# A transposing load for two chunks of x, and two weight loads moved to ScalarE's queue, in the start of a two-problem attention kernel

## Chip, cores, metric

One core of a Trainium2 chip. The metric is the device time of one execution in microseconds (us). "Span" is the time from the first to the last instruction in the profiled execution; it is 1.8 to 2.0 us shorter than the time of the same run. All runs told here were in the fast state (a granted TensorE clock of 0.998 to 1.0 of full speed over the run).

## The reference

Two independent problems A and B with equal shapes, their results side by side:

```python
q = (x @ wq).reshape(B, Sq, Hq, Dh).transpose(0, 2, 1, 3)      # x 16x32x1024, wq 1024x4096
k, v = repeat(k_cache, 8, axis=1), repeat(v_cache, 8, axis=1)  # caches 16x4x512x128
p = softmax(einsum("bhqd,bhkd->bhqk", q, k) * Dh ** -0.5)
out = einsum("bhqk,bhkd->bhqd", p, v).transpose(0, 2, 1, 3).reshape(B, Sq, Hq * Dh) @ wo
```

All data are bfloat16. Here only the first projection of problem A counts: 512 tokens, x split into eight chunks of 128 columns (chunk 0 to 7), and the first eight of 32 heads.

## The kernel before

The projection's matmuls read a chunk of x transposed, 128 columns on the partitions and 512 tokens along the row (128x512 in the trace). Before, chunks 0 to 3 come by plain loads and are transposed on TensorE (four 128x128 blocks each), then copied from PSUM by VectorE or ScalarE; chunks 4 to 7 come by two transposing loads. The queue order is the order of these lines; `NF` is 6, `HC` is 4, `TT` is 4.

```python
load_x(0, TT // 2, TT, nc.scalar)                             # chunks 0, 1, tokens 256..511
nc.scalar.preload_act_table_set("natural_log_exp_and_others")
load_x(0, 0, TT // 2)                                         # chunks 0, 1, tokens 0..255
load_w0(0, 1, 0, NF // 2)       # weights of chunk 0, heads 0..2
load_w0(0, 1, NF // 2, NF)      # weights of chunk 0, heads 3..5
load_w0(1, 2, 0, NF)            # weights of chunk 1
load_x(2, 0, TT)                # chunks 2, 3 of x
load_w0(2, 3, 0, NF)            # weights of chunk 2
load_w0(3, 4, 0, NF)            # weights of chunk 3
load_w0(0, HC, NF, REP)         # heads 6, 7 of chunks 0..3
# ... later loads cut
warm_up(22)                     # idle matmuls until x is there
for k, ts in enumerate(((0, TT // 2), (TT // 2, TT))):
    transpose_x(0, *ts, nc.vector.tensor_copy)
    transpose_x(1, *ts, nc.scalar.copy, spare[k])
for ts in ((0, TT // 2), (TT // 2, TT)):
    first_heads(range(0, NF // 2), (0,), *ts)     # six 256-column matmuls
first_heads(range(NF // 2, NF), (0,))             # three of 512 columns
first_heads(range(0, NF - 2), (1,))
transpose_x(2, 0, TT, nc.vector.tensor_copy)
transpose_x(3, 0, TT, nc.scalar.copy)
first_heads(range(NF - 2, NF), (1,))
first_heads(range(NF), (2, 3))
# ... then heads 6 and 7 of chunks 0..3, chunks 4..7, and the long stream of scores and projections
```

Of the kernel before, what the change touches and what calls it, by code (L numbers as in the profile page):

```python
# [16 lines left out]
P = 128  # L17
# [164 lines left out]
def kernel(  # L182
# [14 lines left out]
    nc = tc.nc  # L197
# [5 lines left out]
    TT = NTOK // P  # L203
# [14 lines left out]
    def fast_path(ok_i):  # L218
        with ExitStack() as fctx:
# [17 lines left out]
            def blk_tile(shape, name, dtype=BF16):  # L237
                return blk.tile(shape, dtype, name=name, tag="blk")
# [215 lines left out]

            NF = REP - 2
            HC = DC // 2
            x_sb = blk_tile([P, TT, HC * P], "x_sb")
            xT[0] = blk_tile([P, DC, NTOK], "xT")
            qT[0, 0] = blk_tile([P, B, REP, SQ], "qT")
            w0 = [blk_tile([P, HC, REP * DH], "w0_sb") for _ in range(2)]  # L460
            x_v = A_x.flatten_outer_dims().rearrange("(t p) d -> p t d", p=P)
            wq_v = A_wq.rearrange("(c p) n -> p c n", p=P)

            def load_x(d0, t0, t1, eng=nc.sync):
                eng.dma_start(
                    out=x_sb[:, t0:t1, d0 * P:(d0 + 2) * P],
                    in_=x_v[:, t0:t1, d0 * P:(d0 + 2) * P],
                )

            def load_x_transposed(d0):  # L470
                nc.sync.dma_start_transpose(
                    out=xT[0][:, d0:d0 + 2, :],
                    in_=A_x.flatten_outer_dims()[:, d0 * P:(d0 + 2) * P],
                )

            def load_w0(d0, d1, h0, h1):
                nc.sync.dma_start(
                    out=w0[d0 // HC][:, d0 % HC:(d1 - 1) % HC + 1, h0 * DH:h1 * DH],
                    in_=wq_v[:, d0:d1, h0 * DH:h1 * DH],
                )  # L480

            load_x(0, TT // 2, TT, nc.scalar)
            nc.scalar.preload_act_table_set("natural_log_exp_and_others")
            load_x(0, 0, TT // 2)
            load_w0(0, 1, 0, NF // 2)
            load_w0(0, 1, NF // 2, NF)
            load_w0(1, 2, 0, NF)
            load_x(2, 0, TT)
            load_w0(2, 3, 0, NF)
            load_w0(3, 4, 0, NF)  # L490
            load_w0(0, HC, NF, REP)
            load_w0(HC, HC + 1, 0, REP)
# [27 lines left out]
            def transpose_x(d, t0, t1, copy, ps=None):  # L520
                if ps is None:
                    ps = psum.tile([P, NTOK], BF16, name="xT_ps", tag="ob")
                for tt in range(t0, t1):
                    nc.tensor.transpose(  # L524
                        ps[:, tt * P:(tt + 1) * P], x_sb[:, tt, d * P:(d + 1) * P], ident[:]
                    )
                ts = slice(t0 * P, t1 * P)
                copy(out=xT[0][:, d, ts], in_=ps[:, ts])

            def first_heads(heads, dcs, t0=0, t1=TT):  # L530
                ts = slice(t0 * P, t1 * P)
                for dc in dcs:
                    for h in heads:
                        nc.tensor.matmul(  # L534
                            first_q[h][:, ts],
                            lhsT=w0[dc // HC][:, dc % HC, h * DH:(h + 1) * DH],
                            rhs=xT[0][:, dc, ts],
                            start=(dc == 0 and t0 == 0),
                            stop=(dc == DC - 1),
                        )  # L540
# [5 lines left out]
            for ts in ((0, TT // 2), (TT // 2, TT)):  # L546
                first_heads(range(0, NF // 2), (0,), *ts)
            first_heads(range(NF // 2, NF), (0,))
            first_heads(range(0, NF - 2), (1,))
            transpose_x(2, 0, TT, nc.vector.tensor_copy)  # L550
            transpose_x(3, 0, TT, nc.scalar.copy)
            first_heads(range(NF - 2, NF), (1,))
            first_heads(range(NF), (2, 3))
            first_q += [psum.tile([P, NW], FP32, name="q_ps", tag="ob")[:] for _ in range(2)]
            first_heads(range(NF, REP), range(HC))
            first_heads(range(REP), range(HC, DC - 1))
            for n, h in enumerate((0, 2, 4, 6, 5, 7, 1, 3)):
# [3 lines left out]
                    out=qT[0, 0][:, :, h, :],  # L561
                    in_=first_q[h].rearrange("p (b s) -> p b s", s=SQ),
# [91 lines left out]
            for k, (lim, op) in enumerate(((1.0 / SUM_HI, ALU.is_ge), (1.0 / SUM_LO, ALU.is_le))):  # L654
                nc.vector.tensor_scalar(
                    out=flags, in0=rall[0:QD].rearrange("p j n -> p (j n)"),
# [18 lines left out]
    ok_i = flag.tile([1, 1], I32, name="ok_i")  # L675
    total = 2 * 2 * NG * QW
    ok = fast_path(ok_i)
    with tc.If(ok < total, preferred_fallthrough_block=True, label="general"):
        general_path(tc, problems, out_flat)
# [30 lines left out]
```

## Time and profile before

| | before |
|---|---|
| time, median (first three runs, then all six of the comparison) | 343.63, then 343.60 us (343.02 to 343.73) |
| profiled run | 343.01 us, span 341.22 us |
| TensorE busy | 335.2 us, 98% of the span |
| chunk 4's first matmul starts at | 12.00 us |

### The profile page before, as it was taken

What the parts mean: (1) busy time and instruction counts of PE and PEld (TensorE: products, weight loads), DVE (VectorE), ACT (ScalarE), POOL (GpSimd) and SP (SyncE); (2) the same over time, 40 slices, a digit from 0 to 9 for tenths busy, and PEclk for the clock granted to TensorE, in tenths of its full rate; (3) what the DMA queues carried; (4) which work ended last, traced back from release to release, by engine and by line L of the source; (5) the groups of instructions that cost most, each with busy time, mean ns of one, the idle gap of its engine ahead of it and who ended that gap; (6) DMA issues with size and microseconds to landing.
All of it is one profiled execution on the core that took longest, in us unless ns stands there. A gap on an engine that the chain in (4) does not pass through costs nothing.

```text
span 341.2 us, 5454 instructions
## 1 busy us (share of the span) xinstructions
PE 335.2 (98%) x2082; PEld 213.6 (63%) x2121; DVE 265.5 (78%) x336; ACT 185.9 (54%) x209; POOL 46.7 (14%) x206
## 2 busy tenths in 40 slices
PE   8999999999999999999999999999999999999996
PEld 6455666666666666666666666666666666666555
DVE  1046988888988898888888988879888888889540
ACT  3058666666667667666645545555555555555110
POOL 0001110011111111110012221222122101111100
PEclk9999999999999999999999999999999999999999
DMA  7999999999996987899999955998449997430001
GB/s 211 287 190 273 285 249 202 233 242 268 291 248 154 232 242 219 210 314 299 308 306 258 250 125 144 334 268 242 118 103 296 356 187 176 104 97 16 18 18 33
DMA packets 128094, 71.70 MB, mean 210 GB/s; under 512 B 75840, under 2 KB 127296, under 8 KB 128064
## 3 DMA queue, kind: packets, MB, share of 16 engines
q1 hardware_dynamic: 127264, 70.07, 84.1%
q0 software_dynamic: 384, 1.05, 0.9%
q8 instruction: 17, 0.28, 0.3%
q10 hardware_dynamic: 416, 0.20, 0.2%
q14 instruction: 13, 0.11, 0.1%
HBM read 50.86 MB, written 2.10 MB: 155 GB/s over the span
## 4 chain that ended last, share of the span: by engine, by line
PE 98%; issue 1%; ACT 0%; ACTq 0%
PE f_ps L320 32%; PE q_ps L301 28%; PE ob L425 17%; PE s_ps L357 16%; PE q_ps L534 4%; PE q_ps L516 1%; PE xT_ps L524 0%; ACT o_sb L329 0%; ACTq L329 0%
## 5 line engine op out<-in xcount | busy, mean ns | idle before, releaser
L365 ACT ACTIVATE p_sb<-s_ps,shift 128x1024 bf16<-128x1024 f32 x128 | 142.7, 1115 | 97.5 <-PE s_ps L357 88.1
L376 DVE TRANSPOSE_TENSOR_REDUCE parts<-p_sb 128x32 f32<-128x1024 bf16 x128 | 158.7, 1240 | 21.0 <-ACT p_sb L365 19.3
L320 PE MATMUL f_ps<-wo_sb,oT 128*128 128x512 bf16 (+1 forms) x525 | 128.2, 366 | 0.6
L301 PE MATMUL q_ps<-xT,wq_sb 128*128 128x512 bf16 x430 | 113.2, 379 | 0.5
L425 PE MATMUL ob<-p_sb,v_sb 128*128 128x256 bf16 x512 | 76.8, 273 | 0.8
L357 PE MATMUL s_ps<-qT,kT 128*128 128x256 bf16 x512 | 76.8, 273 | 0.0
L320 PEld LDWEIGHTS <-oT 128*128 128x128 bf16 x544 | 53.2, 98 | 35.3
L357 PEld LDWEIGHTS <-kT 128*128 128x128 bf16 x512 | 56.9, 113 | 28.3
L301 PEld LDWEIGHTS <-wq_sb 128*128 128x128 bf16 x448 | 43.8, 98 | 32.2
L425 PEld LDWEIGHTS <-v_sb 128*128 128x128 bf16 x512 | 50.1, 98 | 20.0
L447 DVE TENSOR_TENSOR oT<-r,ob 128x512 bf16<-128x512 f32 x64 | 43.9, 686 | 19.9 <-PE ob L425 19.4
L411 DVE STREAM_TRANSPOSE r<-rall 128x512 f32<-128x512 f32 x64 | 44.2, 691 | 1.1
L309 ACT CAST qT<-q_ps 128x512 bf16<-128x512 f32 x56 | 32.7, 583 | 16.5 <-PE q_ps L301 16.5
L394 POOL COPY half<-cs 64x32 f32<-64x32 f32 x32 | 6.5, 204 | 231.8 <-DVE cs L384 231.8
L329 ACT CAST o_sb<-f_ps 128x512 bf16<-128x512 f32 (+1 forms) x17 | 9.5, 559 | 23.6 <-PE f_ps L320 23.6
L534 PE MATMUL q_ps<-xT,w_sb 128*128 128x512 bf16 (+1 forms) x65 | 14.4, 379 | 0.1
L384 DVE TENSOR_REDUCE cs<-parts 128x32 f32<-128x128 f32 x32 | 12.1, 377 | 1.1
L406 DVE RECIPROCAL rall<-sums 128x32 f32<-128x32 f32 x32 | 10.2, 319 | 3.3 <-POOL sums L403 3.3
L534 PEld LDWEIGHTS <-w_sb 128*128 128x128 bf16 x67 | 6.8, 102 | 7.0 <-DMA w_sb<-in_A_wq_dram 0.2
L560 DVE CAST qT<-q_ps 128x512 bf16<-128x512 f32 x4 | 2.5, 684 | 10.2 <-PE q_ps L534 10.2
L331 POOL DMA_DIRECT2D out_dram<-o_sb x8 | 4.6, 574 | 29.3 <-ACT o_sb L329 29.3
L395 POOL TENSOR_TENSOR half<-half,cs 64x32 f32<-64x32 f32 x32 | 7.8, 243 | 2.6
(25 smaller groups left out, 44.7 us busy)
## 6 DMA issues: line engine op xcount, KB each, us to landing
v_sb<-in_A_v_cache_dram SPq DMA_DIRECT2D x16, 512.0 KB, 5.7
wq_sb<-in_B_wq_dram SPq DMA_DIRECT2D x8, 1024.0 KB, 5.7
wo_sb<-in_A_wo_dram SPq DMA_DIRECT2D x8, 1024.0 KB, 7.4
v_sb<-in_B_v_cache_dram SPq DMA_DIRECT2D x16, 512.0 KB, 4.7
wo_sb<-in_B_wo_dram SPq DMA_DIRECT2D x8, 1024.0 KB, 8.1
wq_sb<-in_A_wq_dram SPq DMA_DIRECT2D x5, 1024.0 KB, 5.8
wq_sb<-in_A_wq_dram SPq DMA_DIRECT2D x2, 512.0 KB, 6.7
kT<-in_A_k_cache_dram SPq DMA_TRANSPOSE x64, 4.4
```

The costliest lines, as they stand in the source:

```text
L301: nc.tensor.matmul(ps[:], lhsT=w[:, dc, (h % 4) * DH:(h % 4 + 1) * DH], rhs=xT[pr][:, dc, :], start=(dc == 0), stop=(dc == DC - 1),)
L309: nc.scalar.copy(out=qT[pr, g][:, :, hl, :], in_=ps[:].rearrange("p (b s) -> p b s", s=SQ),)
L320: nc.tensor.matmul(ps[:, 0:width], lhsT=oT[pr, tt][:, h, :], rhs=wo_tiles[pr, nh, h // REP][:, h % REP, off:off + width], start=(h == 0), ...
L357: nc.tensor.matmul(s_ps[:, c, :], lhsT=kT[:, i % GRP, c, :], rhs=qT[pr, g][:, b, :, :].rearrange("p h s -> p (h s)"), start=True, stop=True,)
L365: nc.scalar.activation(out=p_sb[:], in_=s_ps[:], func=ACTF.Exp, bias=shift[:], scale=SCALE)
L376: nc.vector.tensor_reduce(out=parts[k][:, q, :, :].rearrange("p c h -> p (c h)"), in_=st[i]["p"][:].rearrange("p c (h s) -> p (c h) s", s=SQ),
L384: nc.vector.tensor_reduce(out=cs[:], in_=parts.pop(k)[:].rearrange("p q c h -> p q h c"), axis=AX.X, op=ALU.add,)
L406: nc.vector.reciprocal(out=rall[:, k, :], in_=quad.pop(k)[:])
L411: nc.vector.transpose(out=r[:].rearrange("p n s -> p (n s)"), in_=rall[:, k, o * 2 * REP:(o + 1) * 2 * REP] .unsqueeze(2).to_broadcast([P, ...
L425: nc.tensor.matmul(ob[j][:, q, :], lhsT=v_sb[:, i % GRP, c, :], rhs=st[i]["p"][:, c, :], start=(c == 0), stop=(c == KC - 1),)
L447: nc.vector.tensor_tensor(out=out, in0=rcp.pop(j)[:].rearrange("p (q h) s -> p q h s", h=REP), in1=ob.pop(j)[:].rearrange("p q (h s) -> p ...
L534: nc.tensor.matmul(first_q[h][:, ts], lhsT=w0[dc // HC][:, dc % HC, h * DH:(h + 1) * DH], rhs=xT[0][:, dc, ts], start=(dc == 0 and t0 == 0 ...
```

## The change

The intent: take eight transposes off TensorE, which is the bound. Chunks 2 and 3 come transposed by the DMA. Since that load keeps SyncE busy longer, ScalarE issues the weights of chunks 1 and 2.

```diff
-load_w0(1, 2, 0, NF)
-load_x(2, 0, TT)
-load_w0(2, 3, 0, NF)
+load_w0(1, 2, 0, NF, nc.scalar)
+load_x_transposed(2)
+load_w0(2, 3, 0, NF, nc.scalar)
 load_w0(3, 4, 0, NF)
 ...
-first_heads(range(0, NF - 2), (1,))
-transpose_x(2, 0, TT, nc.vector.tensor_copy)
-transpose_x(3, 0, TT, nc.scalar.copy)
-first_heads(range(NF - 2, NF), (1,))
-first_heads(range(NF), (2, 3))
+first_heads(range(NF), (1, 2, 3))
```

The rest of the diff halves `x_sb` to two chunks, so that `load_x` no longer names one, and gives `load_w0` an engine argument.

More of the change, by code (lines that the diff above doesn't have):

```diff
@@ L456, in fast_path @@
             HC = DC // 2
-            x_sb = blk_tile([P, TT, HC * P], "x_sb")
+            x_sb = blk_tile([P, TT, 2 * P], "x_sb")
             xT[0] = blk_tile([P, DC, NTOK], "xT")
@@ L462, in fast_path, with load_x @@
             wq_v = A_wq.rearrange("(c p) n -> p c n", p=P)
-            def load_x(d0, t0, t1, eng=nc.sync):
-                eng.dma_start(
-                    out=x_sb[:, t0:t1, d0 * P:(d0 + 2) * P],
-                    in_=x_v[:, t0:t1, d0 * P:(d0 + 2) * P],
-                )
+            def load_x(t0, t1, eng=nc.sync):
+                eng.dma_start(out=x_sb[:, t0:t1, :], in_=x_v[:, t0:t1, 0:2 * P])
             def load_x_transposed(d0):
@@ L474, in load_x_transposed, with load_w0 @@
                 )
-            def load_w0(d0, d1, h0, h1):
-                nc.sync.dma_start(
+            def load_w0(d0, d1, h0, h1, eng=nc.sync):
+                eng.dma_start(
                     out=w0[d0 // HC][:, d0 % HC:(d1 - 1) % HC + 1, h0 * DH:h1 * DH],
@@ L480, in load_w0 @@
                 )
-            load_x(0, TT // 2, TT, nc.scalar)
+            load_x(TT // 2, TT, nc.scalar)
             nc.scalar.preload_act_table_set("natural_log_exp_and_others")
-            load_x(0, 0, TT // 2)
+            load_x(0, TT // 2)
             load_w0(0, 1, 0, NF // 2)
             load_w0(0, 1, NF // 2, NF)
-            load_w0(1, 2, 0, NF)
-            load_x(2, 0, TT)
-            load_w0(2, 3, 0, NF)
+            load_w0(1, 2, 0, NF, nc.scalar)
+            load_x_transposed(2)
+            load_w0(2, 3, 0, NF, nc.scalar)
             load_w0(3, 4, 0, NF)
```

## The prediction

> **What bounds the kernel now.** I read the page first (busy shares, then the chain that ended last), then the chain and the timeline of the first 25 us, since the change touches nothing later, then the landing time of each early load.
>
> The busy line and the chain of the page:
>
> ```profile
> PE 335.2 (98%) x2082; PEld 213.6 (63%) x2121; DVE 265.5 (78%) x336; ACT 185.9 (54%) x209; POOL 46.7 (14%) x206
> ...
> PE 98%; issue 1%; ACT 0%; ACTq 0%
> ```
>
> TensorE carries 98% of the chain of a 341.2 us span. So a microsecond taken off TensorE's work, or put before it as a wait, in the first 10 us moves the end by that microsecond, unless a later wait takes it back. The chain in the first 25 us, in order of time (start, length, what):
>
> ```profile
> 3.45 0.92 PE xT_ps L524 x8
> 4.37 2.58 PE q_ps L534 x13
> 6.95 0.45 PE xT_ps L524 x8
> 7.40 0.05 issue
> 7.45 10.76 PE q_ps L534 x49
> ```
>
> All pieces are work; the one hole is 0.05 us. The third piece is what the change deletes: the eight transposes of chunks 2 and 3 of x (counting from 0). The first eight (chunks 0 and 1) stay. Next, the loads in the timeline (start, length of the issue, queue), with the rows of the engines that use them:
>
> ```profile
> 0.74 0.45 SPq L465 DMA_DIRECT2D x_sb<-in_A_x_dram  x1
> 0.82 0.46 ACTq L465 DMA_DIRECT2D x_sb<-in_A_x_dram  x1
> 1.26 1.39 SPq L477 DMA_DIRECT2D w_sb<-in_A_wq_dram  x3
> 1.31 1.28 ACT L483 ACT_TABLE_LOAD   x1 [1.31 <-PEq L694]
> 2.69 0.43 SPq L465 DMA_DIRECT2D x_sb<-in_A_x_dram  x1
> 3.17 2.00 SPq L477 DMA_DIRECT2D w_sb<-in_A_wq_dram  x4
> 5.21 1.52 SPq L471 DMA_TRANSPOSE xT<-in_A_x_dram  x1
> 5.79 0.67 PEld L534 LDWEIGHTS <-w_sb 128*128 128x128 bf16 x4 [0.20 <-DMA w_sb<-in_A_wq_dram]
> ```
>
> SyncE issues one plain load every 0.47 us, a transposing load of the same 256 KB in 1.52 us. The last row is the weight load of chunk 1: it came 0.20 us late behind its DMA, but the matmul before was still running, so TensorE lost nothing. The start is just in time: every load lands shortly before its use. From the trace, landing against need (us from the start of the span):
>
> - weights of chunk 0, heads 0 to 2: 3.92 against 4.06
> - weights of chunk 0, heads 3 to 5: 5.03 against 5.17
> - weights of chunk 1: 5.75 against 5.79
> - x of chunks 2 and 3: 6.55 against 6.59
> - weights of chunk 2: 7.06 against 7.45
> - weights of chunk 3: 7.77 against 8.77
> - heads 6 and 7 of chunks 0 to 3: 9.13 against 10.06
> - transposed chunks 4 and 5: 11.05 against 12.00
> - transposed chunks 6 and 7: 13.22 against 15.46
>
> [...] the chain's eight cold transposes take 0.92 us with a wait in them, the eight warm ones 0.45 us (56 ns each). What is deleted runs warm, so it is the cheap half.
>
> [...] between 3.5 and 4.7 us the DMA moved 77 to 215 GB/s, against 312 to 389 GB/s between 4.7 and 6.5 us, while SyncE was still feeding it 96 KB per 0.47 us (about 209 GB/s, an estimate from these rows).
>
> [...] at 22.57 us: a semaphore instruction of ScalarE's sequencer runs while its 0.59 us cast, begun at 22.56, is still busy.
>
> **The change, part by part.**
>
> Removed from TensorE: eight transposes. The next matmul started at 7.237; without them it would follow the one at 6.573 by one 512-column slot of 0.216 us, at 6.789. That is 7.237 - 6.789 = 0.45 us. Chunk 2's first matmul then waited 0.02 us for VectorE's copy (7.690 instead of 7.451 + 0.216 = 7.667). Together 0.47 us, all on the path: this is the ceiling of the gain, 0.14% of 343.63 us.
>
> Removed from VectorE and ScalarE: one copy each (0.42 and 0.59 us). Both engines idle 2.7 us before them and about 10 us after, so nothing.
>
> Removed from SyncE: three issues (0.43 + 0.43 + 0.50 us). Added: one transposing load at about 2.22 us, for 1.52 us as its twin shows. The next issue (weights of chunk 3) comes at 3.8 us, against 3.71 before: SyncE's later stream hardly shifts.
>
> Added to ScalarE: two issues of 0.45 us. If its sequencer runs on past the 1.28 us table load, as I expect from the 22.57 us case, they go out at about 1.35 and 1.85 us, ahead of the 2.22 and 3.17 us they had. If it waits for the table, at 2.6 and 3.1 us, or only after the transposing load's 1.52 us. ScalarE's next work (copies of chunk 1 at 3.92 us) is not reached either way.
>
> New waits. TensorE now wants chunk 1's second half at once, chunk 2 at 7.22 us instead of 7.69. When does the transposing load land? Ahead of it lie the weights of chunks 0, 1 and 2: 96 + 96 + 192 + 192 = 576 KB, 590 kB. From 3.2 us, where x is nearly in, at 340 GB/s (middle of the good stretch) that is 1.7 us; add 0.4 us for slow packets like those the trace has at 4.1 to 4.6 us: 5.3 us. Then 262 kB at 281 GB/s (what the second transposing load moved while alone, 11.6 to 12.4 us): 0.9 us. Then the last packets' way to the semaphore: 0.7 us (that load's packets ended at about 12.5, it landed at 13.22). Sum 7.0 us, uncertain by 0.5 either way, against 7.22. The first transposing load before had its packets stand for up to 1.2 us until 9.72, when the load ahead of it was ending (landed 9.89): so I let it land about 1 us after the last load ahead, not earlier.
>
> Second new wait: chunk 1's weights, pulled forward, share the DMA engines with chunk 0's second half, whose slack is 0.14 us. I allow 0.1 to 0.3 us of wait.
>
> Sum where ScalarE runs ahead: -0.47 + 0.2 (chunk 0) + 0.1 (transposing load, 0.3 late in one case of three) = about -0.2 us. Where ScalarE waits for its table: chunk 1's weights land 0.4 to 0.9 us late, so -0.47 + 0.4 to 0.9 = 0 to +0.4 us. I weigh 7 to 3: about -0.1 us, so 343.5 us.
>
> **The rivals.**
>
> (a) The full gain, 343.2 us: all loads in time. For it: ScalarE's issues fill the thin stretch at 3.5 to 4.7 us, and the weights of chunks 1 and 2 come sooner. Against it: slacks of 0.04 to 0.14 us and a load that is slow by nature as the new wait.
>
> (b) The transposing load takes the place of what it removes: both old ones needed 5.8 us from issue to landing. From 2.22 us that gives 8.0 us, 0.8 after the need: net +0.35, 344.0 us. Against it: those two queued behind four to six loads that had still to land; this one has fewer bytes ahead.
>
> (c) ScalarE's weights are late (table[...]): landing 3.5 us after an issue at 3.75 is 7.2 us, 1.4 after the need of 5.8: net +0.95, 344.6 us.
>
> (d) The loss is hidden or the gain given back later: chunks 4 and 5 have a slack of 0.95 us, less the 0.47 that TensorE comes sooner, so 0.48; heads 6 and 7 have 0.46. Enough if the stream is not late by half a microsecond; it carries the same bytes, only some 0.2 to 0.3 us slower for the transposed ones.
>
> **Range and chances.** The gain is capped at 0.47 us, the three runs before span 0.17 us: lower end 342.9. The loss is open to about +0.8 (b, half of c): upper end 344.4. Two per cent is 6.9 us; nothing in a 10 us start with waits of at most 1.5 us comes near it: faster 0.01, same 0.98, slower 0.01.
>
> **What would show it.** Right: the first 25 us of the chain have one transposing piece instead of two; ScalarE's two issues stand inside the table load; chunk 2's first matmul starts between 7.2 and 7.6; the transposing load lands between 6.6 and 7.6. Wrong on the high side: a hole of half a microsecond or more in TensorE before chunk 1 (ScalarE's weights) or before chunk 2 (the transposing load), or ScalarE's issues only at 2.6 us or later, or lengthened beyond 0.5 us. Wrong on the mechanism: a new hole after 9 us, at heads 6 and 7 or at chunk 4.

The sum: -0.47 + 0.2 + 0.1, about -0.2 us, against 0 to +0.4 us, weighed 7 to 3, came to about -0.1 us, so 343.5 us. "Cold" and "warm" are before and after the moment at which the trace records the full clock, 5.09 us here: the transposes stand 0.107 us apart before it, 0.056 us after. That ScalarE might issue only after the transposing load (2.22 + 1.52, about 3.75 us, the start of (c) with its +0.95 us and so of part of the upper end) was a possibility; no trace shows it. Two phrases are estimates that rest on its own lines: "slow by nature" in (a) on the 1.52 us issue against 0.43 to 0.50 for a plain one, and "0.2 to 0.3 us slower" in (d) on 281 GB/s against 340 to 389, which for 262 kB is 0.16 to 0.26 us.

## The result

Over six runs each: 343.09 us (342.66 to 343.60) against 343.60 us (343.02 to 343.73). Ratio 0.9989, 95% interval 0.9976 to 1.0002. A ratio here is the mean time of one kernel's fast runs over that of the other's of the same rounds, so not quite the ratio of the medians. The class is "same". The same kernel was run twice more among the experiments, at 0.9999 and 1.0002; the mean of the three ratios is 0.9997, which is -0.1 us. A gain is not established.

The profile after, of its fastest run (342.66 us). The page, busy line and chain:

```profile
PE 336.7 (99%) x2113; PEld 213.0 (62%) x2113; DVE 265.2 (78%) x335; ACT 185.4 (54%) x208; POOL 46.7 (14%) x206
...
PE 99%; ACT 0%; issue 0%; ACTq 0%
```

The chain of the first 25 us, in order of time:

```profile
3.45 0.95 PE xT_ps L521 x8
4.40 0.84 PE q_ps L531 x6
5.24 0.01 issue
5.25 13.36 PE q_ps L531 x61
```

The second piece of transposes is gone. Where it stood the matmuls run on. (TensorE's busy time in the page rises all the same, 335.2 to 336.7 us, because the trace of before lacks some matmul records: 2082 of them against 2121 weight loads, and 2113 of each after. The eight are seen in the weight loads.) The timeline of the queues and the weight loads (start, length):

```profile
0.82 0.46 ACTq L465 DMA_DIRECT2D x_sb<-in_A_x_dram  x1
...
1.25 0.93 SPq L474 DMA_DIRECT2D w_sb<-in_A_wq_dram  x2
1.31 1.28 ACT L480 ACT_TABLE_LOAD   x1 [1.31 <-PEq L687]
1.34 0.94 ACTq L474 DMA_DIRECT2D w_sb<-in_A_wq_dram  x2
2.22 1.33 SPq L468 DMA_TRANSPOSE xT<-in_A_x_dram  x1
...
5.24 4.67 PEld L531 LDWEIGHTS <-w_sb 128*128 128x128 bf16 x23 [0.29 <-DMA w_sb<-in_A_wq_dram]
```

ScalarE's two issues start at 1.34 us, while its table load (1.31 to 2.59) still runs. The transposing load is issued in 1.33 us and lands at 7.19; chunk 2's first matmul starts at 7.23, against 7.69 before. A new wait stands at 5.24: the second half of chunk 0's weights landed at 5.20, against 5.03 before, and TensorE was ready earlier.

Chunk 4 starts at 11.54 instead of 12.00 us, and from there the two traces run in parallel to the end: every score matmul that I compared comes 0.46 us earlier, the span ends 0.45 us earlier. It looks as if this one run had nearly the whole 0.47 us; the account below shows that it hadn't, and the next traces why not every run is as fast.

### The profile page after: what moved, and what is told of

Read it like the earlier page. It is cut to its first block, busy times and chain, and to the rows that moved or that the text cites. A ratio compares the mean times of both kernels' runs of the same rounds, so it can differ in the third digit from the quotient of the medians.

```text
span 340.8 us, 5475 instructions
## 1 busy us (share of the span) xinstructions
PE 336.7 (99%) x2113; PEld 213.0 (62%) x2113; DVE 265.2 (78%) x335; ACT 185.4 (54%) x208; POOL 46.7 (14%) x206
## 4 chain that ended last, share of the span: by engine, by line
PE 99%; ACT 0%; issue 0%; ACTq 0%
PE f_ps L320 32%; PE q_ps L301 28%; PE s_ps L357 16%; PE ob L425 16%; PE q_ps L531 4%; PE q_ps L513 1%; PE xT_ps L521 0%; ACT o_sb L329 0%; ACTq L329 0%
## 5 line engine op out<-in xcount | busy, mean ns | idle before, releaser
L320 PE MATMUL f_ps<-wo_sb,oT 128*128 128x512 bf16 (+1 forms) x544 | 132.3, 366 | 0.0
L301 PE MATMUL q_ps<-xT,wq_sb 128*128 128x512 bf16 x448 | 116.9, 379 | 0.0
L309 ACT CAST qT<-q_ps 128x512 bf16<-128x512 f32 x56 | 32.7, 583 | 16.5 <-PE q_ps L301 16.5
L553 ACT CAST qT<-q_ps 128x512 bf16<-128x512 f32 x4 | 2.1, 599 | 12.3 <-PE q_ps L531 12.3
```

Source lines behind the costliest of these rows:

```text
L301: nc.tensor.matmul(ps[:], lhsT=w[:, dc, (h % 4) * DH:(h % 4 + 1) * DH], rhs=xT[pr][:, dc, :], start=(dc == 0), stop=(dc == DC - 1),)
L309: nc.scalar.copy(out=qT[pr, g][:, :, hl, :], in_=ps[:].rearrange("p (b s) -> p b s", s=SQ),)
L320: nc.tensor.matmul(ps[:, 0:width], lhsT=oT[pr, tt][:, h, :], rhs=wo_tiles[pr, nh, h // REP][:, h % REP, off:off + width], start=(h == 0), ...
```

## The experiments

A common account helps to read them. Between chunk 0's first matmul and chunk 4's stand six 256-column and 29 512-column matmuls. At the full clock they take 0.109 and 0.216 us each from start to start, 6.91 us in all. What a trace shows beyond that is (a) the time from chunk 0's first matmul until TensorE gets its full clock: 256-column matmuls stand 0.21 us apart before and 0.11 us after, so half of that time is extra; the trace records when the clock was granted; (b) the transposes; (c) waits, as the rest. "Wait before" is the hole between the last transpose of chunks 0 and 1 and chunk 0's first matmul. Here for twelve traces, in us:

| kernel | wait before | clock granted at | (a) half clock | (b) transposes | (c) waits | chunk 4 starts | span |
|---|---|---|---|---|---|---|---|
| before | 0.00 | 5.09 | 0.46 | 0.47 | 0 | 12.00 | 341.22 |
| before, again (e11) | 0.00 | 5.44 | 0.68 | 0.47 | 0 | 12.14 | 341.36 |
| changed | 0.01 | 4.64 | 0.22 | 0 | 0.21 | 11.54 | 340.77 |
| changed, again (e4) | 0.49 | 6.13 | 0.78 | 0 | 0 | 12.24 | 341.48 |
| changed, third (e12) | 0.32 | 4.75 | 0.09 | 0 | 1.00 | 12.57 | 341.80 |
| e1 ScalarE's issues alone | 0.06 | 5.29 | 0.53 | 0.47 | 0.90 | 13.03 | 342.24 |
| e2 transposing load alone | 0.00 | 4.65 | 0.28 | 0 | 1.49 | 12.77 | 342.01 |
| e3 eight put back | 0.34 | 5.15 | 0.36 | 0.45 | 0.27 | 12.42 | 341.65 |
| e5 later transposing load | 0.48 | 3.91 | 0 | 0 | 0.83 | 12.28 | 341.51 |
| e7 queues exchanged | 0.00 | 5.05 | 0.47 | 0 | 0.29 | 11.78 | 341.01 |
| e10 chunk 2 held back | 0.00 | 5.12 | 0.51 | 0 | 0.81 | 12.32 | 341.70 |
| e13 one queue | 0.00 | 6.29 | 1.04 | 0 | 0 | 12.15 | 341.39 |

Read with it, the first trace of the change is partly luck. Its start is 0.46 us shorter than before by 0.47 for the transposes and 0.24 for an earlier clock, less 0.21 of new waits and 0.03 because chunk 0 began later: the earlier clock hid the waits.

And when the weights of chunk 0 (heads 0 to 2, heads 3 to 5), 1 and 2 and the transposing load landed:

| kernel | chunk 0, 0-2 | chunk 0, 3-5 | chunk 1 | chunk 2 | chunks 2, 3 of x |
|---|---|---|---|---|---|
| before | 3.92 | 5.03 | 5.75 | 7.06 | 6.55 (plain) |
| before, again | 3.79 | 4.95 | 5.73 | 7.36 | 6.48 (plain) |
| changed | 4.16 | 5.20 | 5.01 | 6.11 | 7.19 |
| changed, again | 4.53 | 5.44 | 4.75 | 5.72 | 6.59 |
| changed, third | 4.52 | 6.25 | 5.10 | 6.51 | 7.37 |
| e7 | 3.94 | 4.25 | 6.12 | 6.36 | 7.22 |
| e10 | 3.83 | 4.80 | 6.66 | 6.68 | 7.63 |
| e13 | 4.03 | 5.00 | 6.07 | 6.64 | 7.68 |

Twelve experiments ran, all with right results, each timed in five rounds (the number e9 is not used). The first four (e1 to e4) shared one chip and its runs of the kernel before (median 343.48), so did e5 to e8 (343.32), and e10 to e12 (343.47); e13 came last (343.30).

### e1: ScalarE's issues alone

```diff
 # on the kernel before
-load_w0(1, 2, 0, NF)
+load_w0(1, 2, 0, NF, nc.scalar)
 load_x(2, 0, TT)
-load_w0(2, 3, 0, NF)
+load_w0(2, 3, 0, NF, nc.scalar)
```

> The kernel before with one part of the change: ScalarE issues the weights of chunks 1 and 2; x of chunks 2 and 3 is still a plain load and is still transposed on TensorE. Theory (the gain is the 0.47 us of the removed transposes and their wait, the two issues only make it possible): nothing is gained, the eight transposes still stand in TensorE's row for 0.45 us, first score matmul at 22.3 to 22.6 us as before, time within 0.2 us of before. Rival (the earlier weights are the gain): first score matmul 0.3 us or more earlier, 343.1 us or less.

Measured: 344.12 us, ratio 1.0021 (1.0007 to 1.0035). Slower by 0.7 us, which neither theory said. The timeline of TensorE's weight loads:

```profile
4.22 0.99 PEld L534 LDWEIGHTS <-w_sb 128*128 128x128 bf16 x6
6.29 1.19 PEld L534 LDWEIGHTS <-w_sb 128*128 128x128 bf16 x7 [1.09 <-DMA w_sb<-in_A_wq_dram]
```

Chunk 0's second half landed at 6.25, not 5.03, while chunk 1's weights, which nobody wants before 5.8, were there at 4.74. Moving the two issues to ScalarE is by itself a loss: it put a later need ahead of an earlier one.

### e2: the transposing load alone

```diff
 # on the changed kernel
-load_w0(1, 2, 0, NF, nc.scalar)
+load_w0(1, 2, 0, NF)
 load_x_transposed(2)
-load_w0(2, 3, 0, NF, nc.scalar)
+load_w0(2, 3, 0, NF)
```

> The changed kernel with all weights issued by SyncE again (chunk 1's ahead of the transposing load, chunk 2's behind it). Theory: the transposing load goes out at about 2.7 us and blocks SyncE for 1.3 to 1.5 us, so chunk 2's weights are issued at about 4.1 instead of 1.83 us and land at 7.5 to 7.9, 0.3 to 0.7 after the need of 7.22: nearly the whole gain is lost, 0 to -0.2 us against before. Rival (the transposing load alone is the gain, ScalarE's issues are decoration): as the changed kernel, first score matmul at 21.9, -0.4 us.

Measured: 343.44 us, ratio 0.9999 (0.9985 to 1.0013). That is what the theory said, but no proof of it: the changed kernel had 0.9999 too (e4), so by the times ScalarE's issues gain nothing over this kernel. Its trace (343.79 us, one of its two slowest runs) shows a larger wait than foreseen:

```profile
5.87 0.98 PEld L531 LDWEIGHTS <-w_sb 128*128 128x128 bf16 x6 [0.53 <-DMA w_sb<-in_A_wq_dram]
8.44 0.11 PEld L531 LDWEIGHTS <-w_sb 128*128 128x128 bf16 x2 [1.59 <-DMA w_sb<-in_A_wq_dram]
```

Chunk 2's weights, issued at 4.08 behind the 1.33 us of the transposing load, landed at 8.40 and held up chunk 2. In this order the wait moves from chunk 0 to chunk 2. Chunk 0's second half came in time here (4.88), with the transposing load and all weights on one queue.

### e3: eight transposes put back

```diff
 # on the changed kernel
-first_heads(range(NF), (1, 2, 3))
+first_heads(range(NF - 2), (1,))
+# for d in 0, 1: four nc.tensor.transpose of x_sb into an idle PSUM tile
+first_heads(range(NF - 2, NF), (1,))
+first_heads(range(NF), (2, 3))
```

> The changed kernel with eight idle transposes (of x chunks 0 and 1, into PSUM that nobody reads) put back where the removed ones stood; right results. Theory (TensorE's row is full and the transposing load lands in time): the eight cost their 0.45 us in full, first score matmul at 22.3 to 22.4, no gain left against before (-0.1 to +0.1 us). Rival (the transposing load sets the start of chunk 2, TensorE has slack before it): they fit into a wait and cost under 0.1 us, -0.4 us against before.

Measured: 343.55 us, ratio 1.0006 (0.9992 to 1.0020), against 0.9999 for the changed kernel. The chain has the eight as a piece of their own, with work on both sides:

```profile
5.70 1.68 PE q_ps L531 x7
7.38 0.45 PE idle_ps L550 x8
7.83 11.65 PE q_ps L531 x54
```

The transposing load had landed at 6.81, before the piece began: TensorE was not waiting for it, so the eight cost their 0.45 us. The times agree in sign (0.2 us) but their intervals overlap; it is the trace that shows the size.

### e4 and e12: the changed kernel again

> The changed kernel unchanged, for its spread and a second trace. Theory: -0.3 to -0.6 us against before; chunk 2's first matmul between 7.1 and 7.7 us, and where it is late the transposing load or chunk 0's second half of weights is what it waited for. Rival (the difference is chance of the profile): -0.1 us or less, first score matmul at 22.2 or later.

> The changed kernel once more, for a third trace and more times. Theory: -0.1 to -0.4 us against before (mean of the two earlier sets: -0.4 and 0.0); waits for the weights of chunks 0 and 1 of 0.2 to 0.6 us in sum, the transposing load landing at 6.5 to 7.3 and binding by at most 0.1 us. Rival: the transposing load itself binds (lands after 7.5).

Measured: e4 343.41 us, ratio 0.9999 (0.9985 to 1.0012); e12 343.67 us, ratio 1.0002 (0.9989 to 1.0016). In e4 the theory missed its -0.3 to -0.6 us and the rival's numbers hold (first score matmul at 22.60); e12 missed its -0.1 to -0.4, and its waits (1.32 us) were over the 0.2 to 0.6 expected. The weight loads of e4:

```profile
4.57 1.41 PEld L531 LDWEIGHTS <-w_sb 128*128 128x128 bf16 x8 [0.54 <-DMA w_sb<-in_A_wq_dram]
6.20 2.47 PEld L531 LDWEIGHTS <-w_sb 128*128 128x128 bf16 x12 [0.22 <-issue]
```

and of e12:

```profile
4.57 0.62 PEld L531 LDWEIGHTS <-w_sb 128*128 128x128 bf16 x6 [0.37 <-DMA w_sb<-in_A_wq_dram]
6.29 2.27 PEld L531 LDWEIGHTS <-w_sb 128*128 128x128 bf16 x12 [1.11 <-DMA w_sb<-in_A_wq_dram]
```

Every wait is for chunk 0's weights. The transposing load landed at 6.59 and 7.37, when chunk 2 was only wanted at about 7.9 and 8.3; it bound in neither. In both the first half of chunk 0 landed at about 4.5 us instead of 3.8 to 3.9, in e12 the second half at 6.25 besides.

### e11: the kernel before again

> The kernel before once more, for a second trace: its first trace was of a run of 343.01 us, below its median of 343.5, and had no wait for weights above 0.05 us. Theory: the spread of 0.9 us between its runs is waits for the early loads too, so a trace of a run at 343.4 or more shows 0.3 to 0.8 us of waits before chunk 4, and the first score matmul comes later by just that. Rival (the spread lies elsewhere, in the later stream or the end): first score matmul within 0.1 us of 22.1, the difference after it. Time against before: 1.000 within 0.0015.

Measured: 343.24 us, ratio 0.9992 (0.9979 to 1.0006). The profiled run took 343.25 us, so not one of the slow ones that the expectation spoke of. It has no wait at all; its 0.14 us over the first trace are the later clock less an earlier x. The weight loads, with the eight transposes in the middle:

```profile
3.99 2.60 PEld L534 LDWEIGHTS <-w_sb 128*128 128x128 bf16 x13
6.71 0.65 PEld L524 LDWEIGHTS <-x_sb 128*128 128x128 bf16 x8
7.32 1.25 PEld L534 LDWEIGHTS <-w_sb 128*128 128x128 bf16 x7
```

Not one row has a wait. What the runs of the kernel before at 343.6 to 343.9 do differently was not traced.

### e7 and e8: other splits between the queues

```diff
 # e7, on the changed kernel
-load_w0(0, 1, NF // 2, NF)
-load_w0(1, 2, 0, NF, nc.scalar)
+load_w0(0, 1, NF // 2, NF, nc.scalar)
+load_w0(1, 2, 0, NF)
 # e8: both of these by nc.scalar
```

> The changed kernel with two loads exchanged between the queues: ScalarE issues the second half of chunk 0's weights (then chunk 2's), SyncE chunk 1's. Issue times of all four and the bytes stay. New theory from the second trace of the changed kernel (its gain is partly given back because chunk 1's weights, issued at 1.35 us, run ahead of and beside chunk 0's, which are needed first): chunk 0's second half lands at 4.4 to 4.9 instead of 5.2 to 5.7, TensorE waits under 0.1 us in chunk 0, chunk 2 starts at 6.9 to 7.2, -0.5 to -0.8 us against before and a smaller spread. Rival (the early loads are as slow whichever of them stands first): chunk 0 waits 0.2 to 0.6 us as in the changed kernel, 0 to -0.4 us.

> As e7, but ScalarE issues all three (second half of chunk 0, chunk 1, chunk 2) and SyncE the transposing load at once after the first half of chunk 0, at 1.75 us. Theory: chunk 0 as in e7; the transposing load lands at 6.0 to 6.6 and has slack, but it now runs beside chunk 1's and 2's weights, whose landing decides: if they land by 5.7 and 6.9 it is as e7. Rival ([...]ScalarE's second and third issue are longer than 0.6 us): chunk 1's weights land after 6 us, a wait of 0.3 us or more before chunk 1, 0 to -0.3 us against before.

Measured: e7 342.92 us, ratio 0.9990 (0.9976 to 1.0003); e8 344.30 us, ratio 1.0027 (1.0013 to 1.0040). In e7 chunk 0's second half landed at 4.25 and TensorE had no wait in chunk 0, as the theory said; but chunk 1's weights, now second in turn, landed at 6.12, 0.3 us late. The wait moved one load on, and the times missed the -0.5 to -0.8 us and the smaller spread (0.87 us). The median is the best of all kernels, yet the interval includes 1 and it does not differ from the changed kernel's 0.9989.

e8 tripped over something else. Its queue of ScalarE and the wait for chunk 1:

```profile
1.34 2.89 ACTq L474 DMA_DIRECT2D w_sb<-in_A_wq_dram  x3
...
6.42 0.98 PEld L531 LDWEIGHTS <-w_sb 128*128 128x128 bf16 x6 [0.92 <-DMA w_sb<-in_A_wq_dram]
```

The three issues are not 2.89 us of work: the first two end at 2.28, the third starts at 3.90. In the program built for e8 the third waits for the semaphore of the first load, ScalarE's of x, which landed at 3.88. (It has eight such semaphores for these loads; in the traces of before and of the change, too, the first eight loads name one each and the ninth, issued at 4.19 and 4.22 us, names as its wait that of ScalarE's load of x.) Chunk 2's weights then landed at 10.06. Chunk 1's landed after 6 us (6.38), as the rival said, but not for its reason: neither a plain issue (0.45 us) nor the transposing one (1.33 us) was longer beside the other.

### e6: chunk 1 of x transposed by the DMA too

```diff
 # on e8's loads; x_sb holds chunk 0 alone
+load_x_transposed(1, 1)          # ahead of load_w0(1, 2, ...)
-    transpose_x(1, *ts, nc.scalar.copy, spare[k])
```

> Chunk 1 of x by a transposing load too (x_sb has chunk 0 alone, four cold transposes and two copies fewer), queues as in e8, the transposing loads of chunk 1 and of chunks 2 and 3 one after the other on SyncE. Theory: four cold transposes less are 0.43 us of TensorE, and x's plain load has half the bytes and lands 0.1 to 0.4 us earlier; chunk 1 is then wanted at about 5.2 us, and its transposing load, issued at 1.75, lands at 4.8 to 5.6: -0.5 to -1.1 us against before. Rival (a transposing load is too slow for this place): it lands after 6 us, and chunks 2 and 3 after 7.3, and the gain is no more than e7's.

Measured: 344.06 us, ratio 1.0014 (1.0000 to 1.0027). x's plain load landed at 2.80 and 3.02, 0.4 to 0.7 us earlier than before, and chunk 0 started earlier, but the transposing load of chunk 1 landed at 6.48 and chunks 2 and 3 at 7.86. The rival holds.

### e5: the transposing load one place later

```diff
 # on the changed kernel
-load_x_transposed(2)
 load_w0(2, 3, 0, NF, nc.scalar)
 load_w0(3, 4, 0, NF)
+load_x_transposed(2)
```

> The changed kernel with the transposing load issued one place later on SyncE, behind chunk 3's weights (at 2.7 instead of 2.22 us). It measures the slack of the transposing load, which landed at 7.19 in one trace (need 7.22) and at 6.59 in the other (need 7.49). Theory: it lands 0.5 to 0.8 us later, at 7.2 to 7.9, so the loss is 0 to 0.6 us against the changed kernel, and there is a hole before chunk 2. Rival (it has slack of 0.8 us, only chunk 0's weights bind): under 0.1 us.

Measured: 343.72 us, ratio 1.0014 (1.0000 to 1.0028). The load landed at 7.93, and no hole stands before chunk 2 (last matmul of chunk 1 at 7.74, next at 7.97), because chunk 0's second half came at 5.96 and had made TensorE late already. So e5 does not measure the slack that it was to measure. It is a fourth draw of the same wait for chunk 0.

### e10: chunk 2's weights held back

```diff
 # on the changed kernel
-load_w0(1, 2, 0, NF, nc.scalar)
+load_w0(1, 2, 0, NF)
 load_x_transposed(2)
+for _ in range(3):
+    nc.vector.memset(w0[0][:, 2, 0:NF * DH], 0.0)   # only to delay the next issue
 load_w0(2, 3, 0, NF, nc.scalar)
```

> The changed kernel with chunk 1's weights back on SyncE (issued at about 2.2 us, behind both halves of chunk 0) and chunk 2's on ScalarE but held back until about 2 to 2.5 us by three fills of its destination on VectorE, which is idle then. So chunk 0 has the DMA engines to itself first, as in the kernel before. Theory (what is given back of the 0.47 us is the wait for chunk 0's and 1's weights, which ScalarE's early issues delay): waits before chunk 2 are under 0.2 us in sum, chunk 2 starts at 7.1 to 7.5, -0.3 to -0.6 us against before. Rival (the sum of the early bytes is late in whatever order): waits of 0.4 us or more, -0.2 us or less.

Measured: 343.49 us, ratio 1.0004 (0.9990 to 1.0018). The rival holds. Chunk 0 came in time (3.83, 4.80), but chunk 1's weights, issued on SyncE at 2.21 as before, landed at 6.66 instead of 5.73 to 5.75, together with ScalarE's load for chunk 2 (issued at 2.47, landed 6.68):

```profile
6.70 1.84 PEld L533 LDWEIGHTS <-w_sb 128*128 128x128 bf16 x10 [1.13 <-DMA w_sb<-in_A_wq_dram]
```

### e13: one queue, in the order of need

```diff
 # on the changed kernel
-load_w0(1, 2, 0, NF, nc.scalar)
-load_x_transposed(2)
-load_w0(2, 3, 0, NF, nc.scalar)
+load_w0(1, 2, 0, NF)
+load_w0(2, 3, 0, NF)
+load_x_transposed(2)
```

> The changed kernel with all weights on SyncE in the order of need: both halves of chunk 0, chunk 1, chunk 2, then the transposing load (issued at about 3.2 us), chunk 3. Theory (a load on the second queue does not wait its turn but takes its share from the load that is needed first; in one queue the loads land in the order of need): chunks 0 and 1 land as in the kernel before (3.8 to 3.9, 4.9 to 5.0, 5.7 to 5.9 us), no wait for them above 0.15 us; the transposing load lands 0.9 to 1.1 us behind chunk 2's weights, at 7.3 to 7.7, and binds by 0.1 to 0.5 us; chunk 3 starts between 8.4 and 8.9. First score matmul at 21.8 to 22.2: 0 to -0.4 us against before, most of the gain of the removed transposes kept. Rival (the start is bound by the sum of early bytes in whatever order and queue): waits of 0.5 us or more as in the changed kernel's second and third trace, first score matmul at 22.4 or later.

Measured: 343.97 us, ratio 1.0021 (1.0007 to 1.0034), slower by 0.7 us (0.2 to 1.2). The first score matmul started at 22.51 us, against 22.36 and 22.50 in the traces of before: later than the theory said, but without the rival's waits of 0.5 us. The profiled run (343.18 us, its fastest) has no exposed wait, yet the times are worse. Chunk 0's weights landed in time, as the theory said; chunk 1's landed at 6.07 instead of 5.7 to 5.9, though nothing shared the engines from a second queue. So sharing is not the only thing that makes a load late here. That run got its clock at 6.29 only, so TensorE wanted everything later. The transposing load landed at 7.68 and chunk 3's weights at 8.94; with a clock at 5.1 us they would have been wanted at about 7.2 and 8.5, by an estimate from column (a). That the other four runs, up to 344.25, waited there is likely from these numbers, but they were not traced. One queue in the right order is no remedy.

## Why the prediction was right, point by point

The measured median lies 0.4 us under the predicted 343.5, inside the range; with the two repeats the effect is -0.1 us, the sum that the prediction worked out. Not every term of that sum holds, so that the numbers meet so closely is partly luck: chunk 0's term alone was 0.2 and measured 0.68 in the mean of three traces, more than the 0.47 removed.

- **The 0.47 us ceiling, all on the path: right.** The eight are gone from the chain, and in e3 they cost 0.45 again. The 0.46 us of the first trace is no measure of it (see the account). The difference of the medians, 0.51 us, is over the ceiling; the interval allows that.
- **ScalarE runs on past its table load: right.** Issues at 1.34 us beside the table load (1.31 to 2.59 us), in every trace of the changed kernel.
- **The transposing load at 7.0, 0.5 either way, binding in one case of three: right on the landing** (7.19, 6.59, 7.37). It cost 0.02 us at most in the first trace and nothing in the others, because of the next point.
- **"I allow 0.1 to 0.3 us of wait" for chunk 0's weights: the mis-sized term.** The three traces show 0.22, 0.49 and 1.32 us (wait before plus waits). The reason given was right, the size a guess, and the first half, which the prediction left out, was late too. With both, and in e4 a later clock, chunk 2 began at 7.93 and 8.25 us in the repeats, outside the 7.2 to 7.6 that were to show the prediction right; the first trace had 7.23. The queue table of the window 3.3 to 4.0 us shows what it comes from; queue q1 is SyncE's, q10 ScalarE's, with packets, MB and share of the 16 engines. Before:

```profile
q1 hardware_dynamic: 126, 0.09, 53.5%
```

and in the changed kernel:

```profile
q10 hardware_dynamic: 125, 0.18, 73.5%
q1 hardware_dynamic: 108, 0.07, 30.8%
```

  The DMA moves nearly three times as much, as the prediction hoped (356 against 130 GB/s). But 0.18 of 0.25 MB is ScalarE's load of chunk 1, and the queue that carries chunk 0's weights, wanted first, gets less than before. In packets the two are near each other, 125 and 108; in the mean ScalarE's carry 1.4 kB and SyncE's 0.65 kB. e7 and e10 show the same with the roles changed: the load that shares is late, by 0.4 and 0.9 us.
- **"The loss is hidden or the gain given back later" (rival d): right to doubt it.** From chunk 4 on, the changed kernel and before need 329.22 to 329.23 us. e10 lost another 0.15 us and e6 0.4 us later on; they are the only ones.
- **Rival (c), late weights of ScalarE: the other way round.** ScalarE's weights of chunk 1 were too early (4.75 to 5.10 us, against 5.75 before), not too late. No issue was seen to hold up one of the other queue: in the trace of before those at 0.74 and 0.82 us overlap, at 0.45 and 0.46 us, and in e8 a plain issue of 0.45 us and the transposing one of 1.33 us ran beside each other, neither longer than alone.
- **What the prediction lacked: the time of the clock grant.** It differs by up to 2.4 us between traces (3.91 to 6.29), for equal kernels too (4.64, 4.75, 6.13), and is worth 0 to 1.04 us in column (a). It also trades against waits: in e4 and e13 the clock came late and the waits within (c) are zero, in e12 it came early and 1.00 us of waits show. Clock and waits together make most of the spread that I traced.
- **Readings of the lines.** The slices that it gives as 77 to 215 and 312 to 389 GB/s reach 236 (4.6 to 4.7 us) and 277 (6.3 to 6.4 us). The hole of 0.05 us in the chain is a matmul that the trace lacks: its weight load stands at 7.24. Neither changes the sum.

So the gain went into waits for chunk 0's weights. Shown: those waits in all three traces of the changed kernel, none in two traces of before, and their growth in e1 where the issues alone were moved. The transposing load is not what delays chunk 0: its second half landed at 4.80 to 5.03 us in the five traces where ScalarE issues no weights before 2.4 us (before twice, e2, e10, e13; the last three with the transposing load) and at 5.20 to 6.25 in the six where it issues chunk 1's and 2's at once (the changed kernel three times, e1, e3, e5). Open: how often a run of before waits, since both its traces were of runs below its median; and whether the true effect is -0.4 or 0 us.

## What to carry to other kernels

When a start is just in time, look at what a second queue does besides saving issue time: here its loads didn't wait their turn but took a share of the engines from the load that was needed first (73.5% against 30.8% between 3.3 and 4.0 us, where that load's queue had 53.5% before). So before moving one, compare what lands in which order with what is needed in which order. Taking work off the bound engine in the start pays only as far as the data come in time; here the way that was chosen to feed it, the second queue, brought 0.2 to 1.3 us of waits against 0.47 us of deleted work. And for effects of a tenth of a per cent, read several traces of the same kernel and split each into work, clock and waits: one trace of each would have "proved" a gain of 0.45 us.

## What the traces show of the clock and of the transposing load

- The clock: with matmuls from 0.93 us on, the twelve traces record the full clock at 3.91 to 6.29 us, so 3.0 to 5.4 us after.
- The transposing load: for the movement the trace of before has 281 GB/s for a transposing load alone (11.6 to 12.4 us) against 277 to 389 GB/s for the plain loads (4.7 to 6.5 us). But the issue of the same 256 KB took 1.33 us against 0.43 us for the plain load, and in e2 that delayed the loads behind it (chunk 2's weights were issued at 4.08 and landed at 8.40 us). Also, packets of the transposing load stood still and ended together: in the changed kernel fourteen that began between 5.22 and 5.59 us ended between 5.91 and 5.96.
